# Two transformer layers on one core: the first Q chunks begin with token tile 0 alone, and Wk is loaded ahead of the third x group

## The chip, the cores and the metric

The kernel runs on one core of a Trainium2 chip. The metric is the device time of one execution in microseconds (us); smaller is better. The engines are TensorE (PE, with its weight loads listed apart as PEld), VectorE (DVE), ScalarE (ACT), GpSimd (POOL) and SyncE (SP), which issues most of the DMAs. PSUM is the memory that PE accumulates into; it has eight banks, and one bank holds 128 x 512 numbers in f32.

## The reference

The input x has 2048 tokens of width 1024, all in bf16. Two layers, with the same weights, are applied in turn:

```python
x = x + _A_ref(_layernorm(x), wqkv, wo)       # attention
x = x + _B_ref(_layernorm(x), w1, b1, w2, b2) # dense, gelu (tanh form), dense
x = x + _A_ref(_layernorm(x), wqkv, wo)
x = x + _B_ref(_layernorm(x), w1, b1, w2, b2)

# _A_ref: 32 heads of 32; token s attends to s, s-2, ..., s-14 (8 places, those below 0 masked)
qkv = x @ wqkv
logits = einsum("bhsd,bhswd->bhsw", q, kg) * scale
o = einsum("bhsw,bhswd->bhsd", softmax(logits), vg)
return o.reshape(B, S, D) @ wo
# _B_ref: gelu(x @ w1 + b1) @ w2 + b2, inner width 3584
```

The layernorm has no weights: mean and variance over the 1024 features, eps 1e-5.

## The kernel before

**Tiling.** The 2048 tokens are 16 tiles of 128 (`x[0]` to `x[15]`), in four groups of four tiles (512 tokens, `T`). Two layers of four groups make eight units of work, n = 0 to 7. For a unit, `gen_qkv` makes queries, keys and values in eight chunks each (`NCH`); a chunk is 128 output features, one PSUM tile `acc`, and eight matmuls (k = 0 to 7), each with a 128 x 128 piece of the weights as the stationary operand and the normalised, transposed tokens `xnT` as the moving one. The weight columns of a chunk are taken with a step of eight (`c::NCH`). The PSUM tiles `acc` are eight, one for each bank, and are used in turn.

**Attention.** DVE multiplies qT by shifted views of kT (`new_prod`, 128 x 4096 elements), adds the products up (`add_prods`), and so on through `logits`, `weights` and `av` to `oT`; `gen_wo` then projects oT by Wo and adds it to x. `gen_ffn1` and `gen_ffn2` follow.

**Order.** PE's instructions stay in program order, since `pe()` chains each to the one before. DVE, ACT and POOL are wrapped in `InOrder`: with `on` set, they stay in program order too; otherwise a scheduler places them. SP issues its DMAs in order; at most eight are on their way at a time, as each waits for the one eight places earlier. `stage` runs a generator and calls side functions at given steps.

**The head of the span**, where the change is. SP issues x[0] and x[1], then the four pieces of Wq (`wq_first`, two k each) with x[2] behind the first and x[3] behind the second, then x groups 1 and 2, then Wk. PE runs 14 warm-up matmuls on zeros. `ln_first` normalises tiles 0 to 3: DVE takes the statistics (two `bn_stats` of 512 columns, one `bn_aggr`), ACT the square root (`std`), DVE the reciprocal and the normalisation to `xn`; PE transposes `xn` into a PSUM bank (`transpose_on_pe`, eight transposes) and ACT or DVE copies it to `xnT`. Statistics of tiles 0 and 1 are both taken before the first reciprocal. Tiles 0 and 1 are transposed first, with the bias b1 (`transpose_bias`) in between and two more warm-up matmuls behind. The first query chunks then run over tiles 0 and 1 together (256 columns), a quarter of k (`kq`, two k) at a time for seven chunks, with the transposes of tiles 2 and 3 put in between; their results are copied to the first half of qT. Chunk 7 follows, then `query(c)` runs all eight chunks again over tiles 2 and 3, then come the eight keys and the eight values over all 512 columns.

`ln_early` normalises the tiles of groups 1 and 2 on DVE in the meantime, eight of them: statistics on DVE, the power -1/2 on POOL, the normalisation on DVE, and then a transposing DMA from SP. The result of group 2 lies in the buffer that later becomes qT of unit 1. `ln_stats_ahead` is another way to the statistics, by two passes on ACT with an accumulated sum (`Identity`, then `Square`); before, it is used for group 3 alone.

The pool of weights `wpool` has five buffers of 1 MB: Wq takes two, Wk two, and Wv's first half the fifth; Wv's second half waits for Wq's first buffer.

Of the kernel before, what the change touches and what calls it, by code (L numbers as in the profile page):

```python
# [9 lines left out]
ALU = mybir.AluOpType  # L10
AX = mybir.AxisListType
BF16 = mybir.dt.bfloat16
# [5 lines left out]
def kernel(  # L18
# [18 lines left out]
    P = 128  # L37
# [37 lines left out]
    iop = ctx.enter_context(tc.tile_pool(name="iop", bufs=1))  # L75
    psum = ctx.enter_context(tc.tile_pool(name="psum", bufs=1, space=PSUM))

    def acc_tile():
        return psum.tile([P, T], F32, name="acc", bufs=8)

# [58 lines left out]
    for k in range(0, KD, 2):  # L139
        load_wq_piece(wq_first[k // (KD // 2)], k)  # L140
        if k < 4:
            load_x(0, 2 + k // 2, 3 + k // 2)

# [35 lines left out]
    def transpose_bias():  # L179
        ps = psum.tile([P, KF], BF16, name="acc", bufs=8)  # L180
        pe(nc.tensor.transpose(ps[:], b1_rows[:], ident[:KF, :KF]))
        return ps


# [11 lines left out]

    def ln_stats_ahead(g):
        junk = lnp.tile([P, D], BF16, name="xn", bufs=3)
        for tt in range(NTT):
            t, mean, var = g * NTT + tt, mv_ahead[:, tt, 0:1], mv_ahead[:, tt, 1:2]  # L200
            less = lnp.tile([P, 1], F32, name="less")
            act.activation(junk[:], x[t][:], ACT.Identity, scale=-1.0 / D, accum_out=less[:])
            act.activation(junk[:], x[t][:], ACT.Square, bias=less[:], accum_out=var)
            pool.tensor_scalar(out=mean, in0=less[:], scalar1=-1.0, scalar2=None, op0=ALU.mult)
            rstd = rstd_ahead[:, tt, :]
            pool.tensor_scalar(out=rstd, in0=var, scalar1=1.0 / D, scalar2=EPS, op0=ALU.mult, op1=ALU.add)
            pool.tensor_tensor(out=rstd, in0=rstd, in1=mhalf[:], op=ALU.pow)

    def ln_norm(t, mv, rstd, xn=None):
# [4 lines left out]

    def transpose_on_pe(xn, out, parts=None):
        pst = psum.tile([P, KD, P], BF16, name="acc", bufs=8)
        for k in range(KD):
            pe(nc.tensor.transpose(pst[:, k, :], xn[:, k * P:(k + 1) * P], ident[:]))
        parts = parts or [act.copy]
        n = KD // len(parts)  # L220
        for h, copy in enumerate(parts):
            copy(out[:, h * n:(h + 1) * n, :], pst[:, h * n:(h + 1) * n, :])
# [7 lines left out]

    first_late = []

    def ln_first():

        xa[0] = new_xnT()
        vec.on = act.on = True
        mvs = {}
        stds = {}

        def stats(tt):  # L240
            st6 = lnp.tile([P, 2, 6], F32, name="stats")
            for h in range(2):
                vec.bn_stats(st6[:, h, :], x[tt][:, h * HALF:(h + 1) * HALF])
            mvs[tt] = lnp.tile([P, 2], F32, name="mv")
            vec.bn_aggr(mvs[tt][:], st6[:])
            stds[tt] = lnp.tile([P, 1], F32, name="std")
            act.activation(stds[tt][:], mvs[tt][:, 1:2], ACT.Sqrt, bias=eps_t[:])

        def norm(tt):
            rstd = lnp.tile([P, 1], F32, name="rstd")  # L250
            vec.reciprocal(rstd[:], stds[tt][:])
            return ln_norm(tt, mvs[tt], rstd)

        stats(0)
        stats(1)
        xn0 = norm(0)
        xn1 = norm(1)
        transpose_on_pe(xn0, xa[0][:, 0, :, :], parts=[act.copy] * 4)
        ps = transpose_bias()
        transpose_on_pe(xn1, xa[0][:, 1, :, :], parts=[vec.tensor_copy] * 2 + [act.copy] * 2)  # L260
        warm_up(2)
        act.copy(b1T[:], ps[:])
        stats(2)
        stats(3)
        for tt in range(2, 4):
            first_late.append((norm(tt), xa[0][:, tt, :, :]))
        vec.on = act.on = False
        act.hold()

    def new_xnT(pool=None):  # L270
# [10 lines left out]

    def qkv_chunk(wts, c, xnT, ps=None, k0=0, k1=KD, t0=0, t1=NTT):
        if ps is None:
            ps = acc_tile()
        for k in range(k0, k1):
            mm(ps[:, t0 * P:t1 * P], lhsT=wts[k // (KD // 2)][:, k % (KD // 2), c::NCH], rhs=xnT[:, t0:t1, k, :],
               start=(k == 0), stop=(k == KD - 1), skip_group_check=t1 - t0 < NTT)
        return ps
# [17 lines left out]

    def gen_qkv(n, defer=False, qk_pool=None, v_late=False, qk_next=None, v_first=False, mix=0):
        g = n % NG
# [4 lines left out]
        if v_first:  # L313
            wv = load_qkv(2)
        wq = wq_first if n == 0 else load_qkv(0)
        if not v_first:
            wk = load_qkv(1)

# [13 lines left out]
        if v_first:  # L332
            yield from values()
            wk = load_qkv(1)
        if n == 0:
            early_tiles = ln_early((1, None), (2, qk_next))
            for _ in range(NTT):
                next(early_tiles)
            wv = load_qkv(2)
            for _ in early_tiles:  # L340
                pass
            load_x(3)
        qT = qk_pool.tile([P, NCH, T], BF16, name="qT")
        first = {}
        for kq in range(4 if n == 0 else 0):
            for c in range(7):
                first[c] = qkv_chunk(wq, c, xnT, first.get(c), kq * (KD // 4), (kq + 1) * (KD // 4), 0, 2)
                if (kq, c) == (2, 3):
                    transpose_on_pe(*first_late.pop(0))
                if (kq, c) == (3, 4):  # L350
                    for done in range(2):
                        act.copy(qT[:, done, 0:2 * P], first[done][:, 0:2 * P])
                    transpose_on_pe(*first_late.pop(0))
                    act.hold()
        if n == 0:
            first[7] = qkv_chunk(wq, 7, xnT, t0=0, t1=2)
        for c in list(first)[2:]:
            act.copy(qT[:, c, 0:2 * P], first[c][:, 0:2 * P])
        kT = qk_pool.tile([P, NCH, HALO + T], BF16, name="kT")
# [5 lines left out]
        def query(c):  # L365
            t0 = 2 if n == 0 else 0
            ps = qkv_chunk(wq, c, xnT, t0=t0)
            act.copy(qT[:, c, t0 * P:], ps[:, t0 * P:])

# [6 lines left out]
        ahead = mix or NCH  # L376
        turns = [(query, c) for c in range(ahead)]
        for c in range(NCH):
# [184 lines left out]
    def ln_early(*groups):  # L563
# [6 lines left out]
        vec.on = True  # L570
        ahead = ln_stats(tiles[0][0])
        for i, (t, xn, xT) in enumerate(tiles):
            mv_rstd = ahead
# [4 lines left out]
            if i + 1 == len(tiles):  # L578
                vec.on = False
            yield  # L580

    def stage(gen, count=None, sides=()):
# [22 lines left out]
    pool.on = True  # L605
    warm_up(14)
    ln_first()
    build_constants()
    with tc.tile_pool(name="early", bufs=1) as early:
        load_x(1)  # L610
        load_x(2)
        stage(gen_qkv(0, qk_next=early), sides=at(14, load_b2))
        q1 = gen_qkv(1, defer=True, qk_pool=early, mix=NCH // 2)
# [59 lines left out]
```

## Time and profile before

| what | value |
|---|---|
| median of 4 runs | 1230.8 us (1230.67 to 1231.75) |
| the profiled execution: its own time | 1231.75 us, the slowest of the four |
| its span in the profile | 1230.0 us, so 1.75 us lie around it |
| PE busy | 1222.3 us, 5723 matmuls |
| DVE, ACT, POOL busy | 864.4, 315.3, 105.5 us |
| DMA | 226.64 MB, mean 184 GB/s |
| PE / DVE busy in 0 to 26 us | 24.01 / 20.60 us |
| PE / DVE busy in 26 to 126 us | 99.88 / 96.36 us |
| PE / DVE busy in 136.5 to 1215 us | 1076.03 / 736.15 us |

Times in the profile are microseconds from the start of the span. A timeline line has the start, the length, the engine, the line of the kernel, the operation, out <- in, shapes and the number of instructions; in brackets stands the idle time of the engine just before, and what ended it. Matmuls are pipelined: the length of one (0.27 us for 256 columns) is more than the distance between two, so the distance has to be taken from a run of them. A line of the view of waits has the sum, the number and the longest of the waits. Line 92 is the helper that records DVE, ACT, POOL and SP work, line 117 the helper of the matmuls, line 218 the transposes.

### The profile page before, as it was taken

Reading aid. Unit: us, or ns where it says so; the run is one execution under the profiler, and the core shown is the slowest. Engines: PE = TensorE matmul, PEld = TensorE weight load, DVE = VectorE, ACT = ScalarE, POOL = GpSimd, SP = SyncE. Lnnn points to the kernel's source line nnn. Section 1 sums busy time; section 2 is a strip of 40 time slices with the busy share of each in tenths; the row PEclk is TensorE's granted clock in tenths of the full one; section 3 lists DMA queues with packets and bytes.
Section 4 is the critical chain, followed back from the end, with each engine's and each line's share of the span. In section 5 each row is a group of like instructions: output and inputs, shape, how many; then the busy total and the mean of one; then the engine's idle time right before and its main releaser. Section 6 shows DMA issues by size and latency. Waiting matters only on the chain.

```text
span 1230.0 us, 13953 instructions
## 1 busy us (share of the span) xinstructions
PE 1222.3 (99%) x5723; PEld 632.9 (51%) x5773; DVE 864.4 (70%) x918; ACT 315.3 (26%) x507; POOL 105.5 (9%) x209
## 2 busy tenths in 40 slices
PE   9999999999999999999999999999999999999998
PEld 7666544456444564445544465444654444444444
DVE  8999896898997999375993759937598797011001
ACT  4343253014310144202441024410244101400310
POOL 3010015010101100100011000010000002000000
PEclk9999999999999999999999999999999999999999
DMA  9954674756647654856457565576664558446441
GB/s 282 309 205 145 179 238 162 201 162 208 215 139 237 182 158 164 233 169 186 152 162 234 171 171 173 154 225 201 171 197 146 187 195 209 149 159 196 155 135 53
DMA packets 220031, 226.64 MB, mean 184 GB/s; under 512 B 68194, under 2 KB 187136, under 8 KB 217920
## 3 DMA queue, kind: packets, MB, share of 16 engines
q1 hardware_dynamic: 214704, 208.69, 56.1%
q0 software_dynamic: 5264, 17.06, 3.7%
q8 instruction: 45, 0.74, 0.2%
q14 instruction: 18, 0.15, 0.0%
HBM read 189.01 MB, written 4.19 MB: 157 GB/s over the span
## 4 chain that ended last, share of the span: by engine, by line
PE 97%; DMA 2%; SPq 0%; issue 0%; DVE 0%
PE acc L117 97%; DMA wt<-in_A_wqkv_dram 1%; DMA x<-in_A_x_dram 1%; SPq L92 0%; DMA wt<-in_A_wo_dram 0%; DVE x L92 0%
## 5 line engine op out<-in xcount | busy, mean ns | idle before, releaser
L117 PE MATMUL acc<-xnT,wt 128*128 128x512 bf16 (+1 forms) x3392 | 720.5, 375 | 0.8 <-DMA wt<-in_A_wqkv_dram 0.7
L117 PEld LDWEIGHTS <-wt 128*128 128x128 bf16 x3392 | 400.7, 120 | 318.9 <-DMA wt<-in_A_wqkv_dram 1.2
L117 PE MATMUL acc<-wt,hT 128*128 128x512 bf16 (+1 forms) x1780 | 386.0, 376 | 2.1
L117 PEld LDWEIGHTS <-hT 128*128 128x128 bf16 x1820 | 178.1, 98 | 209.0
L92 DVE TENSOR_TENSOR big<-big 128x1024 bf16<-128x1024 bf16 (+2 forms) x184 | 244.8, 1359 | 2.2
L92 ACT ACTIVATE hT<-acc,b1T 128x512 bf16<-128x512 f32 x224 | 152.1, 688 | 324.9 <-PE acc L117 324.8
L92 DVE TENSOR_TENSOR big<-qT,kT 128x4096 bf16<-128x4096 bf16 x64 | 143.9, 2284 | 36.4 <-ACT kT L92 35.9
L92 DVE TENSOR_TENSOR tmp<-acc,b2bc 128x512 f32<-128x512 f32 x56 | 38.6, 689 | 162.1 <-PE acc L117 159.0
L92 DVE TENSOR_TENSOR big<-abc,vT 128x4096 bf16<-128x4096 bf16 x64 | 144.6, 2284 | 8.9 <-DMA abc<-a 6.9
L92 ACT CAST qT<-acc 128x512 bf16<-128x512 f32 (+1 forms) x72 | 38.2, 544 | 277.8 <-PE acc L117 277.3
L117 PE MATMUL acc<-wt,oT 128*128 128x512 bf16 x440 | 97.6, 379 | 0.5
L92 DVE BATCH_NORM_STATS2 stats<-x 128x6 f32<-128x512 bf16 x120 | 80.0, 681 | 4.4 <-DMA x<-in_A_x_dram 3.3
L117 PEld LDWEIGHTS <-oT 128*128 128x128 bf16 x448 | 43.9, 98 | 53.0 <-DVE oT L92 0.3
L92 DVE TENSOR_TENSOR x<-acc,big 128x512 bf16<-128x512 f32 (+1 forms) x9 | 5.7, 632 | 90.1 <-PE acc L117 90.0
L92 ACT CAST vT<-acc 128x512 bf16<-128x512 f32 x64 | 37.5, 586 | 100.7 <-PE acc L117 100.7
L92 POOL TENSOR_TENSOR rstd<-mv,eps_t 128x1 f32<-128x1 f32 x56 | 17.5, 313 | 528.2 <-DVE mv L92 528.2
L92 ACT CAST kT<-acc 128x512 bf16<-128x512 f32 x64 | 37.4, 586 | 69.6 <-PE acc L117 69.6
L92 DVE TENSOR_TENSOR x<-acc,x 128x512 bf16<-128x512 f32 x64 | 43.0, 672 | 4.9 <-PE acc L117 4.6
L92 DVE TENSOR_SCALAR xn<-x,mv,rstd 128x1024 bf16<-128x1024 bf16 x52 | 28.4, 546 | 20.1 <-POOL rstd L92 19.9
L92 DVE TENSOR_TENSOR x<-tmp,x 128x512 bf16<-128x512 f32 x56 | 38.6, 689 | 1.4
L92 POOL DMA_DIRECT2D big<-big x24 | 13.3, 564 | 212.8 <-DVE big L92 212.8
L92 POOL TENSOR_TENSOR rstd<-rstd,mhalf 128x1 f32<-128x1 f32 x56 | 31.0, 553 | 4.4
(63 smaller groups left out, 260.4 us busy)
## 6 DMA issues: line engine op xcount, KB each, us to landing
wt<-in_B_w_dram SPq DMA_DIRECT2D x56, 1024.0 KB, 5.7
wt<-in_B_w_dram SPq DMA_DIRECT2D x64, 896.0 KB, 4.8
wt<-in_A_wqkv_dram SPq DMA_DIRECT2D x46, 1024.0 KB, 5.8
wt<-in_A_wo_dram SPq DMA_DIRECT2D x16, 1024.0 KB, 5.1
abc<-a POOLq DMA_DIRECT2D x32, 256.0 KB, 4.7
big<-big POOLq DMA_DIRECT2D x24, 256.0 KB, 3.5
x<-in_A_x_dram SPq DMA_DIRECT2D x16, 256.0 KB, 6.8
out_dram<-x SPq DMA_DIRECT2D x31, 128.0 KB, 1.8
```

The source lines that it names most:

```text
L92: inst = f(*args, **kwargs)
L117: return pe(nc.tensor.matmul(*args, **kwargs))
```

## The change

1. **Loads.** SP issues the second piece of Wq ahead of x[2] and x[3], and Wk between x group 1 and x group 2 (`begin_first`).
2. **Tile 0 alone.** `first_queries` takes the place of `ln_first` and of the first chunks in `gen_qkv`. The reciprocal of tile 0 stands behind one statistic of tile 1; xn of tiles 0 and 1 is written in two halves. Seven accumulators of 512 columns stay open, one PSUM bank each, and the eighth bank (`tr`) serves every transpose. Tile 0 and tile 1 run apart, in 128 columns, for k 0 to 3; together, in 256 columns, for k 4 to 7; tiles 2 and 3 follow in 256 columns, into the same bank. The eighth chunk runs at the end in 512 columns, in the bank `tr`. qT is copied once per chunk, 512 columns wide.
3. **Statistics.** `ln_early` leaves out the last two tiles of group 2. Their statistics come from ACT among the copies of the keys (`ln_stats_ahead`), and their normalisation (`ln_end`) stands on DVE behind the fourth product.
4. **Small moves.** 13 warm-up matmuls in place of 14 and 2; the transpose of the bias behind the first key chunk; the load of b2 earlier; a PSUM pool of its own for the head.

The built program shows where the scheduler puts the rest: on SP, Wv's first half stands between the second and third of the transposing DMAs of group 1, its second half behind the fourth; the transposing DMAs of the last two tiles stand behind three weight loads of unit 1. On DVE, seven products and sums of unit 0 stand ahead of the last two normalisations. From the next group's attention on, each engine has the same instructions in the same order as before.

```diff
-        if k < 4:
-            load_x(0, 2 + k // 2, 3 + k // 2)
+        if k == 2:
+            load_x(0, 2, 4)
...
-    def ln_stats_ahead(g):
+    def ln_stats_ahead(g, t0=0):
+        act.on = g == 2
...
+    def first_queries(qT):
...
+        def some(t0, t1, kq, chunks=range(NCH - 1)):
+            for c in chunks:
+                fresh = c not in acc
+                if fresh:
+                    acc[c] = acc_tile()
+                for k in range(kq * (KD // 4), (kq + 1) * (KD // 4)):
+                    mm(acc[c][:, t0 * P:t1 * P], lhsT=wq_first[k // (KD // 2)][:, k % (KD // 2), c::NCH], rhs=xnT[:, t0:t1, k, :],
+                       start=fresh and k == 0, stop=(k == KD - 1), skip_group_check=True)
+
+        bn(0, 0)
+        bn(0, 1)
+        aggr(0)
+        std(0)
+        bn(1, 0)
+        norm(0, 2)
+        bn(1, 1)
+        aggr(1)
+        transpose_on_pe(xns[0], xnT[:, 0, :, :], [act.copy] * 2 + [lambda *io: (std(1), act.copy(*io))] + [act.copy])
+        some(0, 1, 0)
+        norm(1, 2)
+        transpose_on_pe(xns[1], xnT[:, 1, :, :], [vec.tensor_copy] + [act.copy] * 3)
+        some(0, 1, 1)
+        some(1, 2, 0)
+        some(1, 2, 1)
+        bn(2, 0)
+        bn(2, 1)
+        aggr(2)
+        std(2)
+        bn(3, 0)
+        norm(2)
+        bn(3, 1)
+        aggr(3)
+        std(3)
+        transpose_on_pe(xns[2], xnT[:, 2, :, :], [act.copy])
+        some(0, 2, 2)
+        norm(3)
+        some(0, 2, 3, range(5))
+        transpose_on_pe(xns[3], xnT[:, 3, :, :], [vec.tensor_copy, act.copy])
+        vec.on = act.on = False
+        act.hold()
+        some(0, 2, 3, range(5, NCH - 1))
+        for c in range(NCH - 1):
+            for kq in range(4):
+                some(2, 4, kq, [c])
+            act.copy(qT[:, c, :], acc[c][:])
+        last = psum["acc"].tile([P, T], F32, name="tr", bufs=1)
+        qkv_chunk(wq_first, NCH - 1, xnT, last)
+        act.copy(qT[:, NCH - 1, :], last[:])
...
+    def begin_first(qk_next):
+        s = st[0]
+        load_x(1)
+        s["wk"] = load_qkv(1)
+        load_x(2)
+        s["qT"] = attp.tile([P, NCH, T], BF16, name="qT")
+        first_queries(s["qT"])
+        early_tiles = ln_early((1, None), (2, qk_next))
+        for _ in range(NTT):
+            next(early_tiles)
+        s["wv"] = load_qkv(2)
...
+        on_act = tiles[-2:]
+        tiles = tiles[:-2]
...
+    def ln_end():
+        vec.on = True
+        for tt, (t, xn, xT) in zip((NTT - 2, NTT - 1), ln_rest.pop()):
+            ln_norm(t, mv_ahead[:, tt, :], rstd_ahead[:, tt, :], xn)
+            sp.dma_start_transpose(xT, xn.rearrange("s (k p) -> s k p", p=P))
+        vec.on = False
...
-    warm_up(14)
-    ln_first()
-    build_constants()
...
+            warm_up(13)
+            build_constants()
+            begin_first(early)
...
-        stage(gen_qkv(0, qk_next=early), sides=at(14, load_b2))
+        stage(gen_qkv(0), sides=at(0, transpose_bias) + at(1, ln_stats_ahead, 2, NTT - 2) + at(3, ln_end) + at(6, load_b2))
```

The helpers `bn`, `aggr`, `std` and `norm(tt, parts)` inside `first_queries` record the same operations as before; `norm` with two parts writes xn in two halves of 512 columns.

## The prediction

> **What bounds the kernel now.** The page first: who is busy, and on whom TensorE (PE) waits over the whole span.
>
> ```profile
> PE 1222.3 (99%) x5723; PEld 632.9 (51%) x5773; DVE 864.4 (70%) x918; ACT 315.3 (26%) x507; POOL 105.5 (9%) x209
> PE 97%; DMA 2%; SPq 0%; issue 0%; DVE 0%
> PE acc L117 <- DVE big L92: 1.0, 1, 1.0
> PE acc L117 <- DMA wt<-in_A_wqkv_dram: 0.7, 1, 0.7
> PE acc L218 <- DVE xn L92: 0.2, 1, 0.2
> ```
>
> PE carries the chain for 97% of the span, and its listed waits are all in the first 26 us. The change can only move the time at which the steady stream of 512-wide matmuls begins, and what follows from that. So next comes the timeline of PE at the head of the span (start, length, engine).
>
> ```profile
> 0.98 5.90 PE L117 MATMUL acc<-big 128*128 128x512 bf16 x14 [0.98 <-DVE big L92]
> 7.09 0.62 PE L218 MATMUL acc<-ident,xn 128*128 128x128 bf16 x8 [0.21 <-DVE xn L92]
> 8.86 4.13 PE L117 MATMUL acc<-xnT,wt 128*128 128x256 bf16 x36
> 15.47 9.33 PE L117 MATMUL acc<-xnT,wt 128*128 128x256 bf16 x80
> 25.55 19.65 PE L117 MATMUL acc<-xnT,wt 128*128 128x512 bf16 x90 [0.75 <-DMA wt<-in_A_wqkv_dram]
> 25.55 0.65 PE L117 MATMUL acc<-xnT,wt 128*128 128x512 bf16 x2 [0.75 <-DMA wt<-in_A_wqkv_dram]
> 8.86 0.41 PE L117 MATMUL acc<-xnT,wt 128*128 128x256 bf16 x2
> ```
>
> The first query matmul runs at 8.86. One 256-wide takes (4.13 - 0.27)/35 = 0.110 us. Of the group of 80, four are already key matmuls (512 wide, 0.216 each); then PE waits 0.75 us for the second half of Wk. The fifth key matmul starts at 25.55 and is held 0.06 more by a load in the open (below), so the keys stand as if begun at 25.61 - 4 x 0.216 = **24.75**. That is the mark to beat. Then VectorE (DVE), and the one place downstream where PE meets it:
>
> ```profile
> 3.51 1.29 DVE L92 BATCH_NORM_STATS2 stats<-x 128x6 f32<-128x512 bf16 x2 [2.58 <-DMA x<-in_A_x_dram]
> 13.89 0.69 DVE L92 BATCH_NORM_STATS2 stats<-x 128x6 f32<-128x512 bf16 x1 [0.58 <-DMA x<-in_A_x_dram]
> 29.50 6.69 DVE L92 TENSOR_TENSOR big<-qT,kT 128x4096 bf16<-128x4096 bf16 x3
> 124.89 1.90 PE L117 MATMUL acc<-wt,oT 128*128 128x512 bf16 x6
> 124.96 0.75 DVE L92 TENSOR_TENSOR oT<-big 128x512 bf16<-128x512 bf16 x2
> ```
>
> DVE works from 13.89 to 125.71 (124.96 + 0.75) almost without a gap; PE needs the last oT for the first output projection at 125.7. PE and DVE arrive within 0.3 us of each other. So a gain of PE alone is taken back there, and a delay of either is a delay of all. Both chains must be summed.
>
> **Part 1, the first start.** x0 lands at 3.51; DVE has the moments at 5.04, ACT the root at 5.36. Now the reciprocal stands behind one statistic of x1, not behind both and the aggregate: two halves of xn (0.546 for the whole, so about 0.29 each) end near 6.3 instead of 7.04. The 13 warm-up matmuls (14 took 5.90, 0.425 apart) hold PE until 6.50; eight transposes, 0.45; the first copy follows the first transpose by 0.66 as before (7.09 to 7.75), so k 0 and 1 of tile 0 are ready at 7.55. But the first piece of Wq decides:
>
> ```profile
> wt<-in_A_wqkv_dram SPq DMA_DIRECT2D x1, 512.0 KB, 6.1
> ```
>
> Issued at 1.65, it lands at 7.75, and nothing is moved ahead of it. First matmul at 7.8: 1.05 us earlier. The three dropped warm-ups cost nothing, x0 and this piece cover them.
>
> **Part 2, narrow matmuls.** 28 of 256 columns become 56 of 128 (tiles 0 and 1 apart, k 0 to 3, seven chunks). A 128-wide matmul alone is 0.056 (eight transposes: 0.62 - 0.22, over 7). The weight load is the question; no row has a strided load beside so narrow a matmul:
>
> ```profile
> L117 PEld LDWEIGHTS <-wt 128*128 128x128 bf16 x132 | 14.4, 144 | 0.7 <-issue 0.5
> L218 PEld LDWEIGHTS <-xn 128*128 128x128 bf16 x32 | 2.0, 98 | 0.9 <-DVE xn L92 0.9
> ```
>
> The strided Wq load takes 46 ns longer than a plain one. In the open it costs 0.06: the pair at 25.55 is 0.65 - 0.38 = 0.27 apart instead of 0.216; the pair at 8.86 is 0.03 wider than its 0.110. Hidden, a matmul is 0.056; with nothing hidden 0.056 + 0.06 = 0.116. Loads do overlap matmuls everywhere in this trace, so I take 0.063, just over the load: 56 x 0.063 = 3.5 us against 28 x 0.110 = 3.1. Ends: 3.1 and 6.5. The Trainium skill speaks against this edit ("TensorE: Matmul & The Clock Gate", Back-to-back issue gap): it gives about 81 ns for a sustained pair of load and 128-wide matmul, where the transposes here show 56. An estimate by that page: 4.5 us, and an end 0.2 us later than below.
>
> **Part 3, PE's chain.** First quarter of tile 0: 7.8 to 8.7. Transposes of tile 1 need its xn: std(1) is queued on ACT behind two copies (to 8.05), reciprocal and halves to 8.8, so they end at 9.15. The second Wq piece now goes ahead of x2; it landed at 9.8, less 0.26 MB at the 386 GB/s that the DMA view has in these slices: 9.1. Three quarters of 14 x 0.063 run to 11.8. Tile 2 is later than it was: x2 now lands behind 0.5 MB, 8.4 + 1.36 = 9.76; statistics 1.29, aggregate 0.21, one of x3's two statistics 0.65, reciprocal, norm 0.55: its transposes start at **12.6**. So PE stands idle 0.8 us, a new wait (on DVE xn). From there: transposes 0.45, quarter three 14 x 0.110, five chunks of quarter four 10 x 0.110, transposes of tile 3 (ready at 14.5) to 16.14, four more to 16.58. Its copies: DVE's half starts 0.66 after the first transpose, 0.50 long, to 16.84; ACT's half comes after DVE's (as in before, where ACT's copies of tile 1 began only at 9.0, once DVE's had ended), to 17.5. PE waits 0.3 and 0.2. Then 56 x 0.110 less what ran between, to 23.2; the last chunk 8 x 0.216 = 1.72: keys at 24.9. The bias transpose, now among the keys, adds 0.1: 25.0, **0.25 later** than the mark.
>
> **Part 4, Wk.** Behind 6 MB instead of 7 it lands 1.05 MB / 386 GB/s = 2.7 us before 25.35, by 22.7. The keys start at 24.9: the 0.75 us stall goes, and what is late next is PE itself. x8 to x11 land up to 5.4 us later (2 MB): x8 near 21.8, where DVE takes it at 23.8; covered by 2 us. On SP, Wv's first half passes two transposes, and the last two transposes stand behind three weight loads, with DVE's norms (near 45) later still; the next group's second Wk half queues behind them, but its buffer is free only after the values (near 52). No cost.
>
> **Part 5, DVE's chain.** DVE takes up x4 after its copy of tile 3, at 16.84 instead of 13.89: +2.95. Two tiles leave the early run, 2 x 1.85 = -3.7 (0.71 of its waiting for POOL stays). Their two norms come back among the products: 2 x 0.5. Sum **+0.25**. The four ScalarE passes (about 1.1 us each) lie between kT copies of 0.59 at one per 1.73 us; they delay kT by about a microsecond, and DVE, busy with 2.28 us products, doesn't ask sooner. Pool change of PSUM: key chunk 0 waits for copies long done; nothing.
>
> **Sum.** Both chains +0.25 at 125.7, nothing altered behind. The profiled execution (1231.75, the slowest of four; span 1230.0 and 1.75 around it) would become 1232.0; against the median of 1230.8, about **1231.1**. About 0.2% (2.5 us) is what a measurement of this kernel can tell from no change; this is a tenth of it.
>
> **Rivals.**
> - *The hole closes* (x2 or its norm come early, copies don't wait): up to 0.8 + 0.5 off PE; DVE gains the same, as its copy hangs on PE. Net -1.0: 1229.8. Even with no idle at all PE needs 7.8 + 3.1 + 84 x 0.110 + 1.72 + 1.35 = 23.2, -1.6, and the 0.3 at 125.7: this change has no way to 2.5 us of gain. For it: DVE has room between 14.5 and 16.3. Against: x2's bytes.
> - *Loads in the open*: 0.116 each, +3.0, less the 0.8 hole: +2.2 on both chains, 1233.2 with the rest. For: the pair at 8.86. Against: loads 0.055 apart elsewhere.
> - *Slower, by the clock*: the first 13 matmuls are 0.425 apart, later ones 0.216, so PE starts at half speed and rises near 6.5, after 5.5 us without a break. Now a hole of 0.85 us (6.95 to 7.8) and narrow work follow. If the rise slips behind tile 2, 56 x 0.107 replaces 3.5: +2.5, less the hole, 1232.8; if it slips behind quarter four as well, 24 x 0.110 more: 1235.4. It is slower by over 0.2% if half speed lasts beyond about 13.5 us. Against: before had holes of 0.2 and 0.2 there and stayed fast; the column of the granted clock reads 1.00 even over the slow matmuls, so the distances must tell. By the same page (Part 1) an idle window of some 3.4 us drops the clock; no hole here is as long.
>
> **Chances.** Forecast 0.64 (1230.4 to 1231.8), hole closes 0.12, loads open 0.13, clock 0.11. Leaving out the lower part of the second and the upper half of the clock's case gives 1229.5 to 1233.2. Faster by over 0.2% would need a sum outside all of these: 0.04. Slower: most of the clock's case and the edge of the open loads, 0.14. Same: 0.82.
>
> **What would show it.** First query matmul at 7.8 (wrong if past 8.3); 128-wide groups at 0.063 each; an idle of about 0.8 before the third transposes, releaser DVE xn; no wait on wt near 25; keys from 25.0; DVE's first product at 28.75; PE's wait at 125.7 unchanged. If keys begin before 24 or after 26.5, Parts 2 or 3 are wrong; if they begin at 25 and the time moves by over 1 us, the DVE chain is.

## The result, and the profile after

| | before | after |
|---|---|---|
| median | 1230.81 us (52 runs, 1230.41 to 1233.04) | 1233.39 us (32 runs, 1232.58 to 1234.02) |
| profiled execution: time, span, around it | 1231.75, 1230.0, 1.75 | 1233.57, 1231.4, 2.17 |

The ratio is 1.0018, with a 95% interval of [1.0013, 1.0023]: the change costs about 2.2 us (1.6 to 2.8), by the medians 2.6. No change at all is excluded, and the boundary of 0.2% lies inside the interval. The forecast of 1231.1 was about 2 us short (1.9 by the ratio, 2.3 by the medians). The range reached up to 1233.2: by the ratio the kernel after takes 1230.81 x 1.0018 = 1233.0, just inside it, and the median of its own runs lies 0.2 us above it.

The page of after, in the lines that answer to those shown of before:

```profile
PE 1221.6 (99%) x5740; PEld 632.3 (51%) x5790; DVE 862.8 (70%) x914; ACT 318.6 (26%) x508; POOL 111.2 (9%) x211
PE 98%; DMA 1%; DVE 0%; issue 0%; SPq 0%; ACT 0%
```

The view of waits, for PE over the whole span:

```profile
PE acc L117 <- DMA wt<-in_A_wqkv_dram: 1.3, 1, 1.3
PE tr L219 <- DVE xn L92: 1.1, 2, 0.9
PE acc L117 <- DVE big L92: 1.0, 1, 1.0
PE acc L117 <- ACT qT L92: 0.7, 1, 0.7
```

PE has no more work than before (1221.6 us busy against 1222.3) and still carries nearly the whole chain. The waits have changed: the 0.7 for Wk is gone, and there are three where there were none or less: 1.3 for the first piece of Wq, 0.9 for a tile's xn, and 0.7 on ACT, which the prediction did not have. The timeline of PE shows where they stand:

```profile
0.98 4.85 PE L117 MATMUL acc<-big 128*128 128x512 bf16 x13 [0.98 <-DVE big L92]
6.02 0.72 PE L219 MATMUL tr<-ident,xn 128*128 128x128 bf16 x8 [0.20 <-DVE xn L92]
8.06 1.08 PE L117 MATMUL acc<-xnT,wt 128*128 128x128 bf16 x14 [1.32 <-DMA wt<-in_A_wqkv_dram]
8.98 0.61 PE L219 MATMUL tr<-ident,xn 128*128 128x128 bf16 x8
9.43 2.76 PE L117 MATMUL acc<-xnT,wt 128*128 128x128 bf16 x42
13.05 0.62 PE L219 MATMUL tr<-ident,xn 128*128 128x128 bf16 x8 [0.86 <-DVE xn L92]
13.51 2.79 PE L117 MATMUL acc<-xnT,wt 128*128 128x256 bf16 x24
16.13 0.61 PE L219 MATMUL tr<-ident,xn 128*128 128x128 bf16 x8
16.58 7.13 PE L117 MATMUL acc<-xnT,wt 128*128 128x256 bf16 x60
23.55 1.89 PE L117 MATMUL tr<-xnT,wt 128*128 128x512 bf16 x8
26.11 1.89 PE L117 MATMUL acc<-xnT,wt 128*128 128x512 bf16 x8 [0.67 <-ACT qT L92]
27.93 0.18 PE L181 MATMUL acc<-ident,abc 28*128 28x28 bf16 x1
28.05 17.27 PE L117 MATMUL acc<-xnT,wt 128*128 128x512 bf16 x79
```

The last queries (23.55, eight of 0.216) are through at 25.28; the keys begin at 26.11. So PE stands still for 0.83; the view lists 0.67 of it, since it counts from the modelled end of the last query (23.55 + 1.89 = 25.44). What ends the wait is the copy of that last query chunk out of its bank, on ACT:

```profile
25.48 0.59 ACT L92 CAST qT<-tr 128x512 bf16<-128x512 f32 x1 [1.14 <-PE tr L117]
```

The eight keys ahead of the bias transposition take 1.73 of the 1.94 until the group at 28.05, and that group is 17.27 - (78 x 0.216 + 0.38) = 0.04 longer than its matmuls: the bias costs 0.25. DVE, and PE where the two meet:

```profile
29.01 4.49 DVE L92 TENSOR_TENSOR big<-qT,kT 128x4096 bf16<-128x4096 bf16 x2
126.43 0.75 DVE L92 TENSOR_TENSOR oT<-big 128x512 bf16<-128x512 bf16 x2
126.53 5.80 PE L117 MATMUL acc<-wt,oT 128*128 128x512 bf16 x25
```

The output projection runs through its 25 matmuls without a wait that the view lists: at 126, PE is no longer held by DVE.

### The profile page after: what moved, and what is told of

Read it like the earlier page. It is cut to its first block, busy times and chain, and to the rows that moved or that the text cites. A ratio compares the mean times of both kernels' runs of the same rounds, so it can differ in the third digit from the quotient of the medians.

```text
span 1231.4 us, 13990 instructions
## 1 busy us (share of the span) xinstructions
PE 1221.6 (99%) x5740; PEld 632.3 (51%) x5790; DVE 862.8 (70%) x914; ACT 318.6 (26%) x508; POOL 111.2 (9%) x211
## 4 chain that ended last, share of the span: by engine, by line
PE 98%; DMA 1%; DVE 0%; issue 0%; SPq 0%; ACT 0%
PE acc L117 98%; DMA x<-in_A_x_dram 1%; DVE stats L92 0%; PE tr L117 0%; SPq L92 0%; PE tr L219 0%; ACT qT L92 0%; DVE xn L92 0%; DVE xnT L92 0%; DVE x L92 0%; DVE mv L92 0%; PE acc L181 0%; DVE rstd L92 0%
## 5 line engine op out<-in xcount | busy, mean ns | idle before, releaser
L117 PE MATMUL acc<-xnT,wt 128*128 128x512 bf16 (+2 forms) x3404 | 719.8, 374 | 2.1 <-DMA wt<-in_A_wqkv_dram 1.3
L92 ACT CAST qT<-acc 128x512 bf16<-128x512 f32 x63 | 36.9, 586 | 275.8 <-PE acc L117 275.8
L92 DVE BATCH_NORM_STATS2 stats<-x 128x6 f32<-128x512 bf16 x116 | 77.5, 680 | 3.8 <-DMA x<-in_A_x_dram 2.8
L117 PEld LDWEIGHTS <-oT 128*128 128x128 bf16 x448 | 43.9, 98 | 52.8
L92 DVE TENSOR_SCALAR xn<-x,mv,rstd 128x1024 bf16<-128x1024 bf16 (+1 forms) x54 | 28.8, 536 | 20.0 <-POOL rstd L92 19.8
```

The lines of the kernel that those rows point to most:

```text
L92: inst = f(*args, **kwargs)
L117: return pe(nc.tensor.matmul(*args, **kwargs))
```

## The experiments

Each kernel was timed beside the kernel before on the same chip, in five to eleven runs of its own. Rows with the same figure for "before beside it" were taken together on one chip; rows with different figures come from different chips. The span is the median over a kernel's runs; "around" is the median time that lies outside it.

| kernel | median us | before beside it | ratio, 95% interval | span | around |
|---|---|---|---|---|---|
| before, again | 1230.89 | 1230.88 | 1.0001 [0.9990, 1.0011] | 1229.1 | 1.77 |
| Wk ahead alone | 1232.02 | 1231.07 | 1.0011 [1.0002, 1.0019] | 1230.2 | 1.78 |
| Wk ahead, two statistics on ACT | 1230.86 | 1231.07 | 0.9998 [0.9990, 1.0007] | 1229.0 | 1.98 |
| after, x[2] early | 1233.14 | 1231.07 | 1.0019 [1.0010, 1.0028] | 1231.0 | 2.17 |
| after, one pool of 7 + 1 | 1239.62 | 1231.07 | 1.0071 [1.0058, 1.0084] | 1237.5 | 2.16 |
| after, last chunk early | 1233.28 | 1230.88 | 1.0018 [1.0009, 1.0026] | 1231.1 | 2.18 |
| after, eight banks by name | 1233.30 | 1230.88 | 1.0018 [1.0009, 1.0027] | 1231.2 | 2.16 |
| after, statistics on DVE | 1233.12 | 1230.88 | 1.0017 [1.0008, 1.0026] | 1231.1 | 2.02 |
| eight banks, statistics on DVE | 1232.51 | 1231.01 | 1.0016 [1.0007, 1.0025] | 1230.6 | 2.02 |
| eight banks, statistics on DVE, tiles 0 and 1 together | 1232.46 | 1231.01 | 1.0012 [1.0003, 1.0021] | 1230.5 | 2.02 |
| eight banks, statistics on DVE, hole filled | 1232.04 | 1231.09 | 1.0008 [0.9999, 1.0017] | 1230.0 | 2.01 |
| the same as the last, bias early | 1232.44 | 1231.09 | 1.0011 [1.0003, 1.0020] | 1230.3 | 2.04 |

The theory: the change loses about 2.4 us of PE's time ahead of the steady keys, in four places (the mark, the hole, the change of pools, the bias). The rivals: DVE's chain at 126 decides and the head doesn't matter; or the moved loads do it.

### The mark: the kernel before, once more

No edit.

> The kernel before, unchanged, for a second profile. Theory that the profiled execution of before was a late one (its 1231.75 us lie 0.9 over the median, and Wk's landing at 25.35 is what varies): this profile has a span of 1228.8 to 1229.3, PE's wait for Wk is 0.2 us or nothing, and the keys run without a break from 23.8, so that the mark to beat was 23.8 to 24.0 and not 24.75. Rival: the wait of 0.75 is always there, and the median differs for another reason; then the span is near 1229.0 with the wait still in it.

The timeline of PE in this execution (1230.73, span 1229.0):

```profile
8.96 4.12 PE L117 MATMUL acc<-xnT,wt 128*128 128x256 bf16 x36
...
13.37 1.92 PE L117 MATMUL acc<-xnT,wt 128*128 128x256 bf16 x16
...
15.57 29.62 PE L117 MATMUL acc<-xnT,wt 128*128 128x256 bf16 x174
```

One group of 174 from 15.57, and no wait for Wk in it. Of the 128 query matmuls, 52 lie ahead of 15.57; the other 76 at 0.110 end at 15.57 + 8.36 = 23.93. There the keys begin, 0.82 us ahead of the mark that the prediction took from the slowest of four executions. Against this execution the sum closes: keys 26.11 - 23.93 = 2.18 later, plus 0.25 for the bias, is 2.43; the spans differ by 1231.4 - 1229.0 = 2.4. The times of the two executions differ by 2.84, the other 0.4 lying outside the span.

That most executions of before run without the stall is inferred from their times, as only two were profiled: of the 52 in the table at the top 36 lie below 1231.2, and eight reach the 1231.75 of the execution with the stall.

### The loads alone

```diff
+        st[0]["wk"] = load_qkv(1)      # before, between x groups 1 and 2
-            wk = load_qkv(1)
+            wk = s["wk"] if n == 0 else load_qkv(1)
```

> The kernel before with one edit: Wk loaded ahead of the third x group. Theory that PE and DVE are bound together near 126: PE's wait of 0.75 us for Wk goes, keys run without a break from 23.8, but DVE's products still begin at 29.5 and PE waits about 1.0 us for oT near 125; time -0.3 to 0 against before. Rival (PE's head alone counts): -0.9, about 1229.9.

1232.02, 1.0 us more than before beside it. The timeline of PE has no wait at 24, but a new one:

```profile
19.80 32.91 PE L117 MATMUL acc<-xnT,wt 128*128 128x256 bf16 x171
53.52 6.69 PE L117 MATMUL acc<-xnT,wt 128*128 128x512 bf16 x30 [0.82 <-DMA wt<-in_A_wqkv_dram]
```

The later x group delays DVE's norms, these the transposing DMAs on SP, and these the loads of the next unit's weights that queue behind them. The chain that ended last shows it: DVE's products to 42.14, SP to 45.02, the load of the weights for 8.46 to 53.48, then PE. As a typical execution of before had no wait at 24, the move takes none away there and brings one at 53. The theory (-0.3 to 0) and the rival (-0.9) both missed this. With the last two statistics on ACT as well (`ln_stats_ahead` and `ln_end` as in the change, on the first chunks of before):

> The kernel before with Wk ahead of the third x group and the last two statistics on ScalarE, without the new first chunks. Theory that both chains have to move: keys from 23.8, DVE's products from 25.8 or when the keys allow it (kT of chunk 0 near 26.2), two norms back later, so DVE gains about 2.5 us and PE 0.9 to 1.0; time -0.9 to -1.2 against before, about 1229.7. Rival (these two edits cost something that the trace of after hides): no gain or a loss.

1230.86, no difference from before, where the first theory had about 1229.7. In the timeline of DVE:

```profile
21.70 1.29 DVE L92 BATCH_NORM_STATS2 stats<-x 128x6 f32<-128x512 bf16 x2 [1.72 <-DMA x<-in_A_x_dram]
26.66 4.49 DVE L92 TENSOR_TENSOR big<-qT,kT 128x4096 bf16<-128x4096 bf16 x2
```

DVE's first product starts at 26.66, where the kernel before, run again, had 29.30: 2.6 us earlier, in spite of the 1.72 it waits for x[8]. By the softmax's result `a` half of this is gone (82.36 against 83.62), as the two norms come back among the products; then DVE waits 2.5 us for `abc` (1.4 in the other), and the last oT is made at 124.92 against 125.04. The keys begin at 23.73 against 23.93. So an earlier DVE gives nothing here, because a wait behind it takes the gain back; that says nothing yet of a later DVE. The loads and statistics of the change, taken together in the kernel before, bring neither gain nor loss. It follows that what the change costs comes from the rest of it, the first chunks with the two pools and the bias.

### The head: bytes or order

Undone alone in after: x[2] and x[3] at their old places.

```diff
-        if k == 2:
-            load_x(0, 2, 4)
+        if k < 4:
+            load_x(0, 2 + k // 2, 3 + k // 2)
```

> The changed kernel with x2 and x3 issued where they were before, x2 behind the first piece of Wq and x3 behind the second. Late-x2 theory (the idle of 0.9 us ahead of the transposes of tile 2 comes from x2 landing at 10.2): x2 lands near 8.9, that idle goes, but PE may wait up to 0.5 for the second Wq piece at 9.4; keys 0.4 to 0.9 us earlier (near 25.4), time 0.4 to 0.9 under the changed kernel. Rival (transposes wait for DVE's own order): idle stays, same time.

1233.14, with the ratio of after (1.0019 against 1.0018). The keys begin at 25.95, where 25.4 was expected. The hole ahead of the third transposes is gone, and PE waits for the second piece of Wq in its place:

```profile
10.24 2.82 PE L117 MATMUL acc<-xnT,wt 128*128 128x128 bf16 x42 [0.57 <-DMA wt<-in_A_wqkv_dram]
12.89 0.61 PE L219 MATMUL tr<-ident,xn 128*128 128x128 bf16 x8
```

The order of the loads only chooses which of them is waited for. What can be chosen is which matmuls stand there, and that was tried last, below.

### The change of pools

The wait for ACT at 26.11 stands where the first PSUM pool ends and the second begins. Three kernels deal with it. First, a single pool of seven `acc` and one `tr` to the end:

```diff
-        with tc.tile_pool(name="psum_first", bufs=1, space=PSUM) as psum["acc"]:
-            psum["bufs"] = NCH - 1
...
-        psum["acc"] = ctx.enter_context(tc.tile_pool(name="psum", bufs=1, space=PSUM))
-        psum["bufs"] = NCH
```

> The changed kernel with one PSUM pool for the whole kernel (seven accumulators and the bank tr), so that no pool is handed over between the last query chunk and the first key. Hand-over theory (the 0.84 us hole ahead of the keys is the wait for the copy out of tr, and it is most of the loss): no wait on ACT qT, keys at 25.3 in place of 26.1, DVE's wait for kT near 66 gone as well, time 0.6 to 0.8 us under the changed kernel, about 1232.7. DVE theory (DVE's later chain sets the time): keys at 25.3 too, but PE waits for oT near 126 instead, time within 0.2 of the changed kernel.

1239.62. The hand-over is gone, but two other things came in, so the run can't give the price of the hand-over. In PE's timeline, and in its waits over the span:

```profile
24.43 1.89 PE L117 MATMUL tr<-xnT,wt 128*128 128x512 bf16 x8
26.16 1.89 PE L117 MATMUL acc<-xnT,wt 128*128 128x512 bf16 x8
```

```profile
PE acc L117 <- DVE tmp L92: 4.5, 1, 4.5
PE acc L117 <- DMA wt<-in_A_wqkv_dram: 1.7, 1, 1.7
```

With seven accumulators PE once waits 4.5 us (from 380 to 384.5) for DVE to empty one. The other thing is that the clock falls twice, for 3.40 us each time: once in the head, told at the end, and once right behind this wait. The view of windows has busy times of PE, PEld, DVE, ACT and POOL, then the granted clock, 1.00 in the windows on either side of this one:

```profile
384.45:387.85 3.40, 3.31 (x8) 1.17 (x8) 3.09 (x6) 0.00 (x0) 1.96 (x4) 0.50 1.11 237
```

Second, the eighth chunk ahead of the last two half chunks, so that its copy is long done when the keys begin:

```diff
+            if c == 5:
+                last = psum["acc"].tile([P, T], F32, name="tr", bufs=1)
+                qkv_chunk(wq_first, NCH - 1, xnT, last)
+                act.copy(qT[:, NCH - 1, :], last[:])
```

> The changed kernel with the eighth query chunk (bank tr) run ahead of the last two half chunks, so that the last copy before the keys comes out of an accumulator and no longer out of tr. If the first accumulator of the second pool lies in tr's bank: no wait ahead of the keys, keys at 25.3, time 0.6 to 0.8 us under the changed kernel. If the second pool waits until the whole first pool is released: the wait stays at 0.7 to 0.85 us, now for the copy out of the accumulator, and the time stays within 0.2 of the changed kernel.

```profile
22.04 1.89 PE L117 MATMUL tr<-xnT,wt 128*128 128x512 bf16 x8
23.76 1.91 PE L117 MATMUL acc<-xnT,wt 128*128 128x256 bf16 x16
26.34 1.89 PE L117 MATMUL acc<-xnT,wt 128*128 128x512 bf16 x8 [0.67 <-ACT qT L92]
```

The same 0.67, now behind the copy of an ordinary accumulator. So the first key chunk waits not for one bank, but until the last copy out of the whole first pool is done. Third, one pool of eight banks with names of their own, `b0` to `b7`, where nothing is handed over (the helpers' lines move: 97, 122, 224):

```diff
-        return psum["acc"].tile([P, T], F32, name="acc", bufs=psum["bufs"])
+        return psum.tile([P, T], F32, name=bank(), bufs=1)   # b0 to b6 in turn, later b0 to b7
```

> The changed kernel with the eight PSUM banks in one pool, taken in turn by name (seven accumulators and the transposes' bank in the head, all eight later), so that nothing is handed over and no bank is missing later. Hand-over theory: no wait on ACT qT ahead of the keys, keys at 25.3, no wait for kT near 66 on DVE, time 0.6 to 0.8 us under the changed kernel, near 1232.7. Rival (DVE sets the time from 29 on): keys at 25.3, but PE waits for oT near 126, and the time stays within 0.2.

```profile
16.42 10.59 PE L122 MATMUL b<-xnT,wt 128*128 128x256 bf16 x76
...
27.06 34.10 PE L122 MATMUL b<-xnT,wt 128*128 128x512 bf16 x156
61.99 4.32 PE L122 MATMUL b<-xnT,wt 128*128 128x512 bf16 x19 [0.83 <-DMA wt<-in_A_wqkv_dram]
```

The keys follow the queries directly, and the time stays: 1233.30. In this execution PE gives 0.83 back at 62, for the second half of the next Wk, and the chain that ended last runs from that load through kT and DVE's products to the output projection at 127.23. SP's timeline shows why it is late:

```profile
42.16 1.60 SPq L97 DMA_DIRECT2D wt<-in_A_wqkv_dram  x3
45.21 10.75 SPq L97 DMA_TRANSPOSE xnT<-qT  x2
56.06 1.08 SPq L97 DMA_DIRECT2D wt<-in_A_wqkv_dram  x2
```

The last two transposing DMAs, which `ln_end` put behind three weight loads, hold SP until 56. This execution (1233.93) lies 0.63 above the median of its kernel, so a typical one need not lose the gain in this way. A wait for weights between 53 and 62 stands in three profiles, each of an execution above its kernel's median (0.82 with Wk ahead alone, 0.83 here, 1.06 with the bias early, below), and in none of the three that follow here and are the fastest of their eleven.

### The statistics on DVE, and both together

```diff
-        on_act = tiles[-2:]
-        tiles = tiles[:-2]
...
-        stage(gen_qkv(0), sides=at(0, transpose_bias) + at(1, ln_stats_ahead, 2, NTT - 2) + at(3, ln_end) + at(6, load_b2))
+        stage(gen_qkv(0), sides=at(0, transpose_bias) + at(6, load_b2))
```

> The changed kernel with all eight early statistics back on DVE. If PE and DVE are bound together at the first output projection: DVE's first product 3.7 us later (near 32.7), the two norms not added later, so oT 2.7 us later, PE waits about 2.5 us for oT near 126, time +2.0 to +2.7, near 1235.8. If PE alone sets the time: same as the changed kernel.

With the two pools of after: 1233.12, as after; the first theory, 2.0 to 2.7 more, fell. DVE is indeed later, by 1.16 at `a` (86.22 against 85.06 in after), but the product that follows the load of `abc` begins 0.39 earlier, since the wait ahead of it shrinks. In after, and then with the statistics on DVE:

```profile
92.89 4.50 DVE L92 TENSOR_TENSOR big<-abc,vT 128x4096 bf16<-128x4096 bf16 x2 [2.08 <-DMA abc<-a]
```

```profile
92.50 4.50 DVE L92 TENSOR_TENSOR big<-abc,vT 128x4096 bf16<-128x4096 bf16 x2 [0.53 <-DMA abc<-a]
```

So this delay of DVE was absorbed. PE at the keys:

```profile
25.43 1.89 PE L117 MATMUL acc<-xnT,wt 128*128 128x512 bf16 x8 [0.67 <-ACT qT L92]
```

With eight banks:

> The changed kernel with both alterations at once: eight PSUM banks for the whole kernel (no pool change) and all eight early statistics on VectorE, with no norms left among the products. Theory A (the hand-over is worth its 0.7 to 0.8 us, and in the run with eight banks alone that gain was given back because the last two transposing DMAs waited for VectorE's late norms, and the second half of the next Wk queued behind them on SP until about 56): without the late norms, SP passes these transposes before 45, the wait for weights near 61 is gone, and the kernel takes 0.6 to 0.9 us less than the changed one, about 1232.5 (1.2 to 1.8 us over the kernel before). Theory B (VectorE's chain at 126 takes it back, whatever comes before): PE waits at 126 by as much as the keys are earlier; 1233.2, as the changed kernel. The keys begin near 25.2 in both.

1232.51, the 1.5 us over before that the first theory named (1.2 to 1.8). SP's timeline has the last two transposing DMAs done at 43.9 and the weights behind them, and PE runs through from the bias on:

```profile
40.52 3.35 SPq L97 DMA_TRANSPOSE xnT<-qT  x2
...
44.59 8.46 SPq L97 DMA_DIRECT2D wt<-in_A_wqkv_dram  x5
```

```profile
15.89 10.59 PE L122 MATMUL b<-xnT,wt 128*128 128x256 bf16 x76
26.41 0.18 PE L186 MATMUL b<-ident,abc 28*128 28x28 bf16 x1
26.53 39.72 PE L122 MATMUL b<-xnT,wt 128*128 128x512 bf16 x183
```

So the hand-over holds PE for 0.8 us. The two profiles can be compared: each is of the fastest execution of eleven, and their first query matmuls begin at 7.52 and 7.50. With eight banks the eight keys ahead of the bias begin at 15.89 + 10.59 - 1.89 = 24.59, against 25.43 with two pools, 0.84 earlier, and the spans are 1229.9 and 1230.7. For the typical execution the price is less sure: the medians differ by 0.6 and the median spans by 0.5, but these kernels ran on different chips, their ratios (1.0016 and 1.0017) hardly differ, and the intervals overlap. That the time kept by PE is also saved at the end is likely, and not shown by the times.

### Tile 0 alone, and the hole filled

```diff
-        some(0, 1, 0)
+        warm_up(2)
         norm(1, 2)
         transpose_on_pe(xns[1], ...)
-        some(0, 1, 1)
-        some(1, 2, 0)
-        some(1, 2, 1)
+        some(0, 2, 0)
+        some(0, 2, 1)
```

> The same with the first queries undone in part: tiles 0 and 1 together in 256-wide matmuls as in the kernel before (28 of 0.110 us instead of 56 of 0.063), two warm-up matmuls between the transposes of tiles 0 and 1; halves still in one bank, Wk still ahead. Theory A (the head is bound by the bytes of x2 and Wq; what tile 0 alone gains at the start it loses in the hole before the third transposes): first query matmul near 8.7, done with 28 by 11.8, the third transposes where they were (12.6 to 13.1), so keys and time within 0.2 us of the run beside it. Theory B (the early start is worth something): keys later by 0.4 us or more, and the time as well.

1232.46, and 1232.51 for the kernel beside it: no difference that these runs can tell, as each ratio (1.0012 and 1.0016) is known to about 0.0009, or 1.1 us. That beginning with tile 0 alone brings something is not shown. In the one profile the first query matmul runs at 9.56 (7.50 beside it), since tile 1's transposes wait 1.15 for its xn, and the keys begin 0.85 later, more than the 0.2 expected; but that execution, at 1233.46, was the slowest of eleven. Then the old order of the work around tile 2's transposes:

```diff
+        some(0, 2, 2, range(4))
         transpose_on_pe(xns[2], xnT[:, 2, :, :], [act.copy])
-        some(0, 2, 2)
+        some(0, 2, 2, range(4, NCH - 1))
```

> The kernel with eight banks and all early statistics on VectorE, and in it four chunks of quarter two of tiles 0 and 1 (8 matmuls of 0.110 us, as in the kernel before) put ahead of the transposes of tile 2, which stood behind a hole of TensorE of 0.4 to 1.0 us. Theory A (the hole is a matter of order: the third Wq piece has landed when the first two quarters are done, as in the kernel before, which ran 36 matmuls ahead of these transposes without a wait): no wait on xn at the third transposes, keys 0.4 to 0.9 us earlier, near 24.3, and the median 0.5 to 0.9 us lower than with eight banks and statistics on VectorE alone (1232.5), about 1231.7. Theory B (bytes: the third piece of Wq lands only after 12.5): the wait on xn is replaced by one for wt, and the time stays at 1232.4 or more.

```profile
8.92 3.59 PE L122 MATMUL b<-xnT,wt 128*128 128x128 bf16 x50
12.34 0.61 PE L224 MATMUL b<-ident,xn 128*128 128x128 bf16 x8
...
25.51 0.18 PE L186 MATMUL b<-ident,abc 28*128 28x28 bf16 x1
```

42 narrow matmuls and 8 of 256 columns run in one group up to the transposes; neither xn nor the third piece of Wq is waited for. The bias stands at 25.51, against 26.41 in the kernel without this edit; 0.25 of these 0.90 are an earlier first query matmul (7.25 against 7.50). The keys ahead of it begin at 23.69 (24.3 expected), 0.24 ahead of the kernel before, run again. So this hole was one of order: the change took away the work that had covered it. This profile (1230.98) is of the fastest of eleven executions. The median is 1232.04 (1231.7 expected), 0.95 over before instead of 1.5, and the span 0.6 less; the interval now includes no change, but it overlaps that of the kernel without the edit, so the gain rests on the trace. What the slower executions still lose is not shown. Last, the bias transposition back to the head (`transpose_bias()` behind `some(1, 2, 1)`):

> The same with the transposition of the bias back at the head, after the second quarter of tile 1, instead of among the keys. Theory A (the small transposition costs 0.25 us of gaps wherever PE streams 512-wide matmuls behind it, and little among the first chunks): no gap at 26, 0.1 to 0.3 us less than the run beside it. Theory B (whatever PE gains at the head, VectorE's last product at 126 takes back): PE waits for oT there by as much, and the time is that of the run beside it.

1232.44, 0.4 more instead of 0.1 to 0.3 less; the profiled execution (1233.26) lost 1.06 at 54.63 waiting for weights. Neither theory is shown by it: the 0.25 of the bias are read in after's timeline, but not shown to be worth their time.

## Where the prediction was right, and where it was wrong

Of the mechanism, the half on PE was right: there is no gain, the keys come later, and the time follows them. The half on DVE, a chain that binds PE wherever either is late, was wrong, and the size was too small. That the range still holds the time, by the ratio, is luck: its upper part stood there for loads in the open and for a slow clock, and neither came; the forecast's own part ended at 1231.8. From keys at the mark to the end the sum had +0.25 in the span, and 2.43 were measured, in four terms:

| step, as the prediction put it | predicted | measured | missed |
|---|---|---|---|
| "the mark to beat": keys as if begun at | 24.75 | 23.93 | 0.82 |
| Part 3: queries done, "keys at 24.9" | 24.9 | 25.28 | 0.38 |
| Part 5: "Pool change of PSUM: key chunk 0 waits for copies long done; nothing" | 0 | 0.83 | 0.83 |
| Part 3: "The bias transpose ... adds 0.1" | 0.1 | 0.25 | 0.15 |

The four make 2.18, and 0.25 + 2.18 = 2.43. Some 0.4 us more lie around the span. The largest two are the mark and the pool change; the sum had put the second at nothing.

**The mark** is the step that failed in its logic. The sum was made against an execution that the text itself called the slowest of four, and was then carried to the median by subtracting the difference. But that difference was the stall: the 0.75 us that the typical execution, by its time, doesn't have. What Part 4 removed, most executions seem never to have paid.

**The pool change** was argued from the copies, and they were not long done: the copy of the last query chunk starts only at 25.48, 0.2 us after PE would be free for the keys, and takes 0.59. The next pool waits for all of the first, as the run with the last chunk early shows.

**Part 1** had the first query matmul at 7.8; it came at 8.06, as the piece of Wq landed later. The warm-ups ended at 5.83, not at 6.50, which changed nothing, as it was the piece of Wq that decided. **Part 3** named the hole, its length of 0.8 and its releaser rightly (0.86, DVE xn), but had it from 11.8 to 12.6, and it stood from 12.19 to 13.05: x[2] landed by 10.26, not at 9.76. The two waits for the copies of tile 3, 0.3 + 0.2, came out as 7.13 - (59 x 0.110 + 0.27) = 0.37.

**Part 2** held: (2.76 - 0.225)/41 = 0.062 for a 128-wide matmul with its strided load, where 0.063 was taken. The Trainium skill ("TensorE: Matmul & The Clock Gate", Back-to-back issue gap) gives about 81 ns for such a pair; here the trace disagrees, and loads in the open (0.116) are refuted as well.

**Part 4** held for the Wk stall, which is gone. "No cost" did not hold in general: in the kernel before, the move alone costs 1.0 us, through the queue on SP that Part 4 had looked at and called free. In the new head it can go either way, with no wait for the next unit's weights in after's profile, and 0.83 and 1.06 us in those with eight banks and with the bias early.

**Part 5's** first product at 28.75 came at 29.01. Its premise, that "a gain of PE alone is taken back there, and a delay of either is a delay of all", fell on both sides: with two pools, a DVE later by 1.16 us at `a` cost nothing, and with eight banks PE's 0.84 us was still there at the end of the span, in one profile of each. The arrival of PE and DVE within 0.3 us at 126 was no proof that both were tight. DVE had waits for `abc` of 0.5 to 2.5 us on its way there, and these can shrink when it is late. And in the profile of before the chain that ended last did not come to 126 through DVE at all, but through the load of Wo, which landed at 125.94, 0.23 after the last oT:

```profile
120.77 5.17 DMA wt<-in_A_wo_dram
```

DVE is not far off, though: with Wk ahead and two statistics on ACT, and in three of the kernels built on after, the chain that ended last does reach the output projection through it. "PE's wait at 125.7 unchanged" was wrong as well: in after that wait is gone, as PE itself comes late.

**The rivals.** The hole did not close by itself. The clock stayed at 1.00 in after. The test that the prediction set ("if keys begin ... after 26.5, Parts 2 or 3 are wrong") was not met with keys at 26.11, and could not have found the mark or the pools.

What stays open: why about 2.15 us lie around the span in after and 1.77 in before. It goes mostly with the kernel, as the runs of before, again, have 1.72 to 1.81 and those of after 2.10 to 2.22; but in others it spreads, from 1.78 to 2.10 with Wk ahead and two statistics on ACT. No experiment took it apart. That a later DVE is absorbed at the load of `abc` is read in one execution only. Nor were the 128-wide matmuls and the copies of tile 3 undone one by one in the last kernel, whose median is still 0.95 over the before beside it, 0.23 of that around the span.

## What to carry to other kernels

A stall in a profiled execution that is late by about as much as the stall is long may belong to that execution alone: before a change is credited with removing it, find the same stall in a typical one. When work is moved ahead, look for what it used to cover: eight matmuls taken from in front of a transpose opened a hole of 0.4 to 0.9 us, up to their own length of 0.88. And a new pool in the place of an old one was here a barrier on the last reader of the old, 0.83 us of PE, whichever buffer that reader held; named banks in a single pool had no such wait.

## Of the hardware

Two things were not expected. In the kernel with one pool of 7 + 1, PE stood still from 6.85 to 8.54, and half a microsecond later the granted clock fell to half. The view of windows of that kernel; behind the engines stand the granted clock, the DMA share and the GB/s:

```profile
5.00:9.00 4.00, 2.31 (x20) 1.16 (x18) 3.07 (x10) 1.67 (x6) 0.00 (x0) 1.00 0.91 312
9.00:12.40 3.40, 3.40 (x36) 3.40 (x34) 1.49 (x3) 0.93 (x3) 0.00 (x0) 0.50 1.05 391
```

After a wait of 1.69 us the clock was at 0.50 for 3.40 us. The kernel after has a wait of 1.32 at the same place, and the kernel with the last chunk early one of 1.47; both kept 1.00, the second with PE busy for only 1.65 of the 4.00 us from 5 to 9, against 2.31 in the row above. Whether the length of the wait decides or its place in time, no run shows. The second fall, in the row shown with that kernel, came behind a wait of 4.52 us and lasted 3.40 as well. The Trainium skill ("TensorE: Matmul & The Clock Gate", Part 1) has the clock judged in free-running windows of about 3.4 us, and the length of both slow stretches agrees; that it takes an idle window of that length to lose the clock agrees with the second fall and not with the first. The kernel after stood closer to the clock rival than "no hole here is as long" had put it.

The other is how much the landing of the same first loads varies, on one chip too: the first query matmul waited for Wq's first piece until 8.48 with the last chunk early, 8.05 with eight banks by name and 7.52 with the statistics on DVE, in one execution each, though nothing ahead of that piece differs between them. Terms of 0.4 us in a head that is bound by its loads are within this.
